# Decayed keys on GpSimd from the seventh tile on, and products of r and k in written order on VectorE

## The chip, the cores and the metric

One NeuronCore of a Trainium2 chip runs the whole program. The metric is the device time of one execution in microseconds (us), lower being better. Engines are called TensorE (PE in the profile), VectorE (DVE), ScalarE (ACT), GpSimd (POOL) and SyncE (SP, which issues the loads and stores).

## The reference

Three layers follow one another on 4 sequences of 768 tokens: a linear attention with decay (8 heads of 48), a gated mixer with a convolution of three taps, and a mixer with layer norm and a residual.

```python
for t in range(S):                                   # attention, S = 768, D = 48
    cur = np.einsum('bhd,bhe->bhde', u[None] * kt, vt)
    y[:, :, t] = np.einsum('bhd,bhde->bhe', rt, state + cur)
    state = w[None, :, :, None] * state + np.einsum('bhd,bhe->bhde', kt, vt)
h = np.maximum(x @ w_in, 0.0)                        # x: 3072 x 384, w_in: 384 x 1024
conv_out = conv_w[0] * h[s-1] + conv_w[1] * h[s] + conv_w[2] * h[s+1]
x = (h / (1 + np.exp(-conv_out))) @ w_out            # w_out: 1024 x 384
xn = (x - mu) / np.sqrt(var + 1e-06) * g_ln
out = x + np.maximum(xn @ w_ch1, 0.0) @ w_ch2        # 384 x 1536 x 384
```

All is float32. The state of the attention after a token is a sum of older keys times values, each weighted by a power of the decay w.

## The kernel before

The tokens are cut into 24 tiles of 128, six to a sequence; tile numbers in the code start at 0, so the seventh tile is n = 6. Within a tile the recurrence becomes matmuls. Per tile these steps are written, and their names are those of the trace:

- `load_tile` (line 224) loads three tensors through SyncE: `kt` (keys by token), `rk` (r and k transposed, 112 x 1024) and `rv` (r and v by token). `rk` and `rv` have three buffers and `kt` two; tile n + 3 is loaded at the end of tile n.
- `decayed_k` (line 244) multiplies the keys by a table and writes `kks`: from the seventh tile on two copies at once, 128 x 768 (line 249), one weighted for the state and one by u. It is called for tile n + 2 at the end of tile n, and `kks` has two buffers, by parity of n.
- `attn_tile` (line 341), first part: the product of r and k with a table of powers, in place on `rk` (line 347, "the product" below); then `av`, the u-weighted keys times r (line 352), its sum over the head (`a`, line 354), and eight ScalarE instructions that put this sum on the diagonal of `aT` (line 358).
- second part: `dot_products` (line 291), eight matmuls of `rk` into `dps`, and two `COPY_PREDICATED` that lay the part of `dps` above the diagonal into `aT` (line 363).
- third part: `products` (line 262), the matmuls into `yps` from state and `aT`; the result is split into a high and a low part `xh` and `xl` (lines 371 and 372), the mixer's input; then the loads and the decayed keys for later tiles.
- `state_update` (line 380): matmuls of `kks` and v into `pst`, and `sn` and `sw`, the new state.

The first six tiles take another way (`light_tile`, line 299) in which the last but one of these parts is spread over GpSimd.

The first mixer works on groups of three tiles: for each of eight blocks of 128 columns nine matmuls into `psm` (weights in a high and a low part, three products of 128 x 128 by 386), ReLU on ScalarE (`h`), the convolution as one ScalarE and two VectorE instructions (`c`, lines 472 and 474), a sigmoid (line 454), a multiply (line 455), and a split into `gh` (ScalarE, line 460) and `gl` (VectorE, line 461). Nine matmuls of these with w_out add up in `acc`, two to three blocks later. The second mixer follows from about 300 us on.

The weights arrive as 64-bit patterns and are decoded on the way (`wjob`, line 139): an absolute value on ScalarE, a clamp on GpSimd (on VectorE for the first four), three integer instructions on VectorE (lines 130 to 135) and a split into a high part (ScalarE: `wih`, `woh`) and a low part (VectorE: `wil`, `wol`). All their instructions carry line 75, that of the helper `InOrder`.

What sets the order: TensorE's instructions are written through `InOrder`, and so keep the order in which they are written. So do the decode's instructions on VectorE, ScalarE and GpSimd among one another (`vo`, `ao`, `go`, lines 78 to 81). Everything that is written with `v_`, `a_` and `g_` is placed by the scheduler of the build, which may move it ahead of or behind other work of its engine.

The attention's parts are put in between the mixer's blocks by `attention` (line 402) and `after1` (line 768); in its steps the first part of tile n + 1 is written after the state update of tile n, and the second part of n + 1 after the third of n.

Of the kernel before, what the change touches and what calls it, by code (L numbers as in the profile page):

```python
# [12 lines left out]
ALU = mybir.AluOpType  # L13
AX = mybir.AxisListType

B, H, S, D = 4, 8, 768, 48
# [21 lines left out]
LIGHT = 6  # L38
# [10 lines left out]
def body(ctx, tc, r, k, v, w, u, w_in, conv_w, w_out, g_ln, w_ch1, w_ch2, rkT, krv, small, out):  # L49
# [13 lines left out]
    v_ = nc.vector  # L63
# [14 lines left out]
    vo = InOrder(nc.vector)  # L78
    ao = InOrder(nc.scalar)
    so = InOrder(nc.sync)  # L80
    go = InOrder(nc.gpsimd)
# [4 lines left out]
    trk = tables_[0:PR, 128:128 + 2 * NP * C].rearrange("x (a p c) -> x a p c", a=2, p=NP)  # L86
# [3 lines left out]
    tku = tables_[:, o + C:o + C + 2 * DM].rearrange("x (a h d) -> x a h d", a=2, h=H)  # L90
# [8 lines left out]
    kks = const.tile([128, 2, 2, H, 64], F32, name="kks")  # L99
# [122 lines left out]
    loaded = {}  # L222

    def load_tile(n):
        if n >= NT:
            return
        rk = io.tile([PR, 2, NP, C], F32, tag="rk", name="rk", bufs=3)
        kt = io.tile([128, DM], F32, tag="k", name="kt", bufs=2)
        rv = io.tile([128, DM + H * 64], F32, tag="rv", name="rv", bufs=3)
        nc.sync.dma_start(out=kt, in_=krv[n, :, 0:DM])  # L230
        nc.sync.dma_start(out=rk.rearrange("x a p c -> x (a p c)"), in_=rkT[n])
        c0 = DM if n < LIGHT else 0
        nc.sync.dma_start(out=rv[:, c0:], in_=krv[n, :, DM + c0:])
        loaded[n] = (rk, kt.rearrange("x (h d) -> x h d", h=H), rv[:, 0:DM].rearrange("x (h d) -> x h d", h=H),
                     rv[:, DM:].rearrange("x (h d) -> x h d", h=H))
# [3 lines left out]
    def new_xT(j):  # L239
        xT[j] = (mp.tile([128, KT, T + 2], F32R, tag="xh", name="xh", bufs=3),  # L240
                 mp.tile([128, KT, T + 2], F32R, tag="xl", name="xl", bufs=3))
        return xT[j]

    def decayed_k(n):

        if n < LIGHT:
            v_.tensor_tensor(out=kks[:, n % 2, 0, :, 0:D], in0=loaded[n][1], in1=tku[:, 0], op=ALU.mult)
            return
        v_.tensor_tensor(out=kks[:, n % 2, :, :, 0:D], in0=loaded[n][1].unsqueeze(1).to_broadcast([128, 2, H, D]), in1=tku,
                         op=ALU.mult)  # L250

    state = [None]
# [9 lines left out]
    def products(n, yps, rT, vt, aT):  # L262
        opened = set()

        def part(g, lhsT, rhs):
            c0 = 32 * (g % 4)
            pe.matmul(yps[c0:c0 + 32, g // 4, :], lhsT=lhsT, rhs=rhs, start=c0 not in opened, stop=True,
                      skip_group_check=True)
            opened.add(c0)

        if n % TPB:
            for g in range(3 * NP):
                p, s_ = divmod(g, 3)
                part(g, sbd[n % 2][:, p, 32 * s_:32 * s_ + 32], rT[:, p, :])
        for parts in zip(*from_heads):
            for g, p, q, c0 in parts:
                pair = vt[:, 2 * p:2 * p + 2, :].rearrange("x a d -> x (a d)")
                part(g, pair[:, c0:c0 + 32], aT[:, q, p, :])

    def halos(n, xh, xl):  # L280
        i, j = n % TPB, n // TT
        for t, e in ((xh, 0), (xl, 1)):
            if i == 0:
                g_.memset(t[:, :, 0:1].bitcast(F32), 0.0)
            if i == TPB - 1:
                g_.memset(t[:, :, T + 1:T + 2].bitcast(F32), 0.0)
            if n % TT == 0 and i > 0:
                g_.tensor_copy(out=xT[j - 1][e][:, :, T + 1:T + 2], in_=t[:, :, 1:2].bitcast(F32))  # L288
                g_.tensor_copy(out=t[:, :, 0:1], in_=xT[j - 1][e][:, :, T:T + 1].bitcast(F32))

    def dot_products(rT, kT):
        dps = [ps_a.tile([128, NP, C], F32, tag="pa", name="dps") for _ in range(2)]
        for p in range(NP):
            for q in range(2):
                q0 = 64 * q
                pe.matmul(dps[q][:, p, :], lhsT=kT[q0:q0 + D, p, :], rhs=rT[q0:q0 + D, p, :], start=True, stop=True)
        return dps

    def light_tile(n, rk, vt, py, py_tag):
# [31 lines left out]
        if n + 2 < NT:  # L331
            decayed_k(n + 2)
# [8 lines left out]
    def attn_tile(n):  # L341
        b, i = divmod(n, TPB)
        rk, _, rt, vt = loaded[n]
        py, py_tag = (ps_c, "acc") if n < EARLY else (ps_a, "pa")

        rT, kT = rk[:, 0], rk[:, 1]
        v_.tensor_tensor(out=rk, in0=rk, in1=trk, op=ALU.mult)  # L347
        if n < LIGHT:
            yield from light_tile(n, rk, vt, py, py_tag)
            return  # L350
        av = ap.tile([128, H, D], F32, tag="av", name="av", bufs=2)
        v_.tensor_tensor(out=av, in0=kks[:, n % 2, 1, :, 0:D], in1=rt, op=ALU.mult)  # L352
        a8 = sp.tile([128, H, 1], F32, tag="a8", name="a8", bufs=2)
        v_.tensor_reduce(out=a8.rearrange("x (q p) o -> x q (p o)", q=2), in_=av.rearrange("x (p q) d -> x q p d", q=2),
                         axis=AX.X, op=ALU.add)
        aT = ap.tile([128, 2, NP, C], F32, tag="aT", name="aT", bufs=2)
        for h in range(H):
            a_.activation(out=aT[:, h // NP, h % NP, :], in_=ident, func=AF.Copy, scale=a8[:, h, :])  # L358
        yield

        dps = dot_products(rT, kT)
        for q in range(2):
            v_.copy_predicated(out=aT[:, q], mask=later.bitcast(I32).unsqueeze(1).to_broadcast([128, NP, C]), data=dps[q])  # L363
        yield

        yps = py.tile([128, KT, C], F32, tag=py_tag, name="yps")
        products(n, yps, rT, vt, aT)
        j = n // TT
        xh, xl = xT[j] if j in xT else new_xT(j)
        sl = slice(1 + (n % TT) * C, 1 + (n % TT) * C + C)  # L370
        a_.activation(out=xh[:, :, sl], in_=yps, func=AF.Copy)
        v_.tensor_tensor(out=xl[:, :, sl], in0=yps, in1=xh[:, :, sl].bitcast(F32), op=ALU.subtract)
        load_tile(n + 3)
        if n + 2 < NT:
            decayed_k(n + 2)
        halos(n, xh, xl)
        finished[0] = n
        yield
# [23 lines left out]
    def attention():  # L402

        tiles = {}

        def go_on(n):
            if 0 <= n < NT:
                next(tiles.setdefault(n, attn_tile(n)), None)

        go_on(0)  # L410
        decayed_k(1)
        go_on(0)
        go_on(1)
        for n in range(NT):
            state_update(n)
            go_on(n - 1)
            if n + 1 != EARLY:
                go_on(n + 1)
            yield
            go_on(n)  # L420
            go_on(n + 2 if n + 1 < EARLY else n + 1)
            yield
# [455 lines left out]
```

## Time and profile before

| | us |
|---|---|
| median of 3 runs (661.33 to 667.29) | 661.51 |
| the profiled execution | 661.62 |
| its span on the core | 659.8 |
| TensorE busy in the span | 627.7 |
| VectorE busy | 416.3 |
| ScalarE busy | 301.8 |
| GpSimd busy | 104.6 |

The profile comes from one execution, taken by the hardware profiler. The span runs from the first to the last instruction; the device time holds 1.8 us more around it. "Busy" is the time in which an engine works on at least one instruction; a share of the whole span is an average over stages that have different limits, so the stretches below are read one by one. A wait is put down to the instruction or load whose end came last before the waiting one began.

### The profile page before, as it was taken

Reading aid. Unit: us, or ns where it says so; the run is one execution under the profiler, and the core shown is the slowest. Engines: PE = TensorE matmul, PEld = TensorE weight load, DVE = VectorE, ACT = ScalarE, POOL = GpSimd, SP = SyncE. Lnnn points to the kernel's source line nnn. Section 1 sums busy time; section 2 is a strip of 40 time slices with the busy share of each in tenths; the row PEclk is TensorE's granted clock in tenths of the full one; section 3 lists DMA queues with packets and bytes.
Section 4 is the critical chain, followed back from the end, with each engine's and each line's share of the span. In section 5 each row is a group of like instructions: output and inputs, shape, how many; then the busy total and the mean of one; then the engine's idle time right before and its main releaser. Section 6 shows DMA issues by size and latency. Waiting matters only on the chain.

```text
span 659.8 us, 11761 instructions
## 1 busy us (share of the span) xinstructions
PE 627.7 (95%) x4782; PEld 574.4 (87%) x4782; DVE 416.3 (63%) x772; ACT 301.8 (46%) x662; POOL 104.6 (16%) x124
## 2 busy tenths in 40 slices
PE   5979699999999999999999999999999999999996
PEld 4868598888988998999998999999999999999995
DVE  6779999999898899877978843413422422422111
ACT  3456868687677778856764521211211221121110
POOL 5464450010001002003115500100100100100000
PEclk9987989999999999999999999999999999999999
DMA  8556716345254332203144303003001101100101
GB/s 250 158 188 208 220 43 208 95 118 160 69 143 158 120 103 63 84 2 132 37 144 132 95 1 96 0 1 96 0 1 49 48 1 49 48 1 13 36 1 52
DMA packets 25295, 56.50 MB, mean 86 GB/s; under 512 B 2961, under 2 KB 15378, under 8 KB 25234
## 3 DMA queue, kind: packets, MB, share of 16 engines
q1 hardware_dynamic: 25234, 55.68, 27.0%
q8 instruction: 39, 0.64, 0.4%
q14 instruction: 22, 0.18, 0.1%
HBM read 46.24 MB, written 9.44 MB: 84 GB/s over the span
## 4 chain that ended last, share of the span: by engine, by line
PE 69%; DVE 14%; DMA 10%; ACT 4%; issue 2%; POOL 1%; SPq 1%; ACTq 0%; DVEq 0%
PE acc L75 32%; PE psm L75 31%; DMA rk<-in_rkT_dram 8%; DVE wdec L75 3%; PE yps L75 3%; DVE c L474 2%; DVE rk L347 2%; ACT aT L358 1%; DVE aT L363 1%; PE pxt L75 1%; PE dps L75 1%; DVE gl L461 1%; DVE c L455 1%; DMA x1b<-x_dram 1%; DVE av L352 1%
## 5 line engine op out<-in xcount | busy, mean ns | idle before, releaser
L488 DVE SCALAR_TENSOR_TENSOR rl<-psm,rh 128x512 fp32r<-128x512 f32 x72 | 49.6, 688 | 132.6 <-ACT rh L487 129.1
L487 ACT ACTIVATE rh<-psm 128x512 fp32r<-128x512 f32 x72 | 43.0, 597 | 186.5 <-PE psm L75 186.5
L75 PE MATMUL acc<-c2h,rh 128*128 128x384 f32 x288 | 97.1, 337 | 0.0
L75 PE MATMUL acc<-c2l,rh 128*128 128x384 f32 x288 | 97.0, 337 | 0.0
L75 PE MATMUL acc<-c2h,rl 128*128 128x384 f32 x288 | 97.0, 337 | 0.0
L75 PE MATMUL psm<-xnh,c1h 128*128 128x512 f32 x216 | 86.5, 401 | 0.0
L75 PE MATMUL psm<-xnh,c1l 128*128 128x512 f32 x216 | 84.9, 393 | 0.0
L75 PE MATMUL psm<-xnl,c1h 128*128 128x512 f32 x216 | 84.8, 393 | 0.0
L474 DVE SCALAR_TENSOR_TENSOR c<-h,tables,c 128x384 f32<-128x384 f32 x128 | 79.4, 626 | 4.8 <-ACT c L472 4.2
L75 PE MATMUL psm<-xh,wih 128*128 128x386 f32 x192 | 69.9, 364 | 4.0 <-DVE aT L363 3.0
L75 PE MATMUL acc<-woh,gh 128*128 128x384 f32 x192 | 66.6, 347 | 3.3 <-ACT woh L75 3.3
L75 PE MATMUL acc<-woh,gl 128*128 128x384 f32 x192 | 65.8, 343 | 3.9 <-DVE gl L461 3.9
L75 PE MATMUL psm<-xl,wih 128*128 128x386 f32 x192 | 67.0, 349 | 2.4 <-POOL xl L288 2.4
L75 PE MATMUL acc<-wol,gh 128*128 128x384 f32 x192 | 65.4, 340 | 1.7 <-DVE wol L75 1.7
L75 PE MATMUL psm<-xh,wil 128*128 128x386 f32 x192 | 66.9, 349 | 0.0
L75 POOL TENSOR_SCALAR wdec<-wdec 128x768 f32<-128x768 f32 (+2 forms) x19 | 54.2, 2851 | 74.2 <-ACT wdec L75 47.4
L75 PEld LDWEIGHTS acc<-c2l,rh 128*128 128x128 f32 x288 | 54.1, 188 | 3.0
L75 PEld LDWEIGHTS acc<-c2h,rh 128*128 128x128 f32 x288 | 54.1, 188 | 2.8
L75 PEld LDWEIGHTS acc<-c2h,rl 128*128 128x128 f32 x288 | 54.1, 188 | 0.0
L511 POOL TENSOR_TENSOR rs<-rs,nhalf 128x1 f32<-128x1 f32 x24 | 16.8, 708 | 210.0 <-DVE rs L510 203.7
L75 PEld LDWEIGHTS psm<-xnh,c1l 128*128 128x128 f32 x216 | 40.6, 188 | 9.2
L75 PEld LDWEIGHTS psm<-xnl,c1h 128*128 128x128 f32 x216 | 40.7, 188 | 6.2
(115 smaller groups left out, 1130.1 us busy)
## 6 DMA issues: line engine op xcount, KB each, us to landing
rk<-in_rkT_dram SPq DMA_DIRECT2D x24, 448.0 KB, 5.0
st<-in_moe_w_ch_dram SPq DMA_DIRECT2D x12, 768.0 KB, 5.9
rv<-in_krv_dram SPq DMA_DIRECT2D x18, 448.0 KB, 4.8
kt<-in_krv_dram SPq DMA_DIRECT2D x24, 192.0 KB, 2.8
x_dram<-x SPq DMA_DIRECT2D x24, 192.0 KB, 1.9
x1b<-x_dram SPq DMA_DIRECT2D x24, 192.0 KB, 3.7
out_dram<-x1b SPq DMA_DIRECT2D x24, 192.0 KB, 2.0
st<-in_moe_w_in_dram SPq DMA_DIRECT2D x6, 512.0 KB, 6.5
```

Source lines behind the costliest of these rows:

```text
L75: return lambda *args, **kw: tc.keep_in_program_order(op(*args, **kw))
L347: v_.tensor_tensor(out=rk, in0=rk, in1=trk, op=ALU.mult)
L352: v_.tensor_tensor(out=av, in0=kks[:, n % 2, 1, :, 0:D], in1=rt, op=ALU.mult)
L358: a_.activation(out=aT[:, h // NP, h % NP, :], in_=ident, func=AF.Copy, scale=a8[:, h, :])
L363: v_.copy_predicated(out=aT[:, q], mask=later.bitcast(I32).unsqueeze(1).to_broadcast([128, NP, C]), data=dps[q])
L455: v_.tensor_tensor(out=st["c"], in0=st["h"][:, 1:T + 1], in1=st["c"], op=ALU.mult)
L461: v_.tensor_tensor(out=st["gl"], in0=st["c"], in1=st["gh"].bitcast(F32), op=ALU.subtract)
L474: v_.scalar_tensor_tensor(out=c, in0=h[:, o:o + T], scalar=cw[:, tap, f:f + 1], in1=c, op0=ALU.mult, op1=ALU.add)
L487: a_.activation(out=gh[:, 0:cols], in_=ps[:, 0:cols], func=AF.Relu)
L488: v_.scalar_tensor_tensor(out=gl_[:, 0:cols], in0=ps[:, 0:cols], scalar=0.0, in1=gh[:, 0:cols].bitcast(F32), op0=ALU.max, op1=ALU.subtract)
L511: g_.tensor_tensor(out=rs[:, 1:2], in0=rs[:, 0:1], in1=nhalf, op=ALU.pow)
```

## The change

The decayed keys of the tiles from the seventh on are written for GpSimd, in written order, in place of VectorE. The product of r and k stays on VectorE, and from the seventh tile on it is written through `InOrder`, so that it keeps its place among VectorE's other written-order instructions (those of the decode).

```diff
         if n < LIGHT:
             v_.tensor_tensor(out=kks[:, n % 2, 0, :, 0:D], in0=loaded[n][1], in1=tku[:, 0], op=ALU.mult)
             return
-        v_.tensor_tensor(out=kks[:, n % 2, :, :, 0:D], in0=loaded[n][1].unsqueeze(1).to_broadcast([128, 2, H, D]), in1=tku,
+        go.tensor_tensor(out=kks[:, n % 2, :, :, 0:D], in0=loaded[n][1].unsqueeze(1).to_broadcast([128, 2, H, D]), in1=tku,
                          op=ALU.mult)
...
         rT, kT = rk[:, 0], rk[:, 1]
-        v_.tensor_tensor(out=rk, in0=rk, in1=trk, op=ALU.mult)
+        (v_ if n < LIGHT else vo).tensor_tensor(out=rk, in0=rk, in1=trk, op=ALU.mult)
         if n < LIGHT:
```

TensorE's order is the same before and after; those of VectorE, ScalarE, GpSimd and SyncE are dealt anew by the scheduler, as the following places show.

VectorE, around the thirteenth tile's `COPY_PREDICATED` (`aT<-tables,dps`), before. `rk<-rk,tables` is the product, L474, L455 and L461 are the mixer's gate:

```order
L455 TENSOR_TENSOR c<-h,c 128x384
L474 SCALAR_TENSOR_TENSOR c<-h,tables,c 128x384
L461 TENSOR_TENSOR gl<-c,gh 128x384
L455 TENSOR_TENSOR c<-h,c 128x384
L372 TENSOR_TENSOR xl<-yps,xh 128x3x128
L347 TENSOR_TENSOR rk<-rk,tables 112x1024
L363 COPY_PREDICATED aT<-tables,dps 128x512 x2
L461 TENSOR_TENSOR gl<-c,gh 128x384
L347 TENSOR_TENSOR rk<-rk,tables 112x1024
L474 SCALAR_TENSOR_TENSOR c<-h,tables,c 128x384
L249 TENSOR_TENSOR kks<-kt,tables 128x16x48
```

The same place of VectorE in the changed order (the product now has line 75, since the helper records it):

```order
L75 TENSOR_TENSOR rk<-rk,tables 112x1024
L352 TENSOR_TENSOR av<-kks,rv 128x384
L455 TENSOR_TENSOR c<-h,c 128x384
L474 SCALAR_TENSOR_TENSOR c<-h,tables,c 128x384
L354 TENSOR_REDUCE a_1898<-av 128x8
L474 SCALAR_TENSOR_TENSOR c<-h,tables,c 128x384
L461 TENSOR_TENSOR gl<-c,gh 128x384
L372 TENSOR_TENSOR xl<-yps,xh 128x3x128
L363 COPY_PREDICATED aT<-tables,dps 128x512 x2
```

Before, the products of the fifteenth and sixteenth tile stand around the thirteenth tile's `COPY_PREDICATED`; now the thirteenth tile's own product stands eight rows ahead of it, with `av` of the fourteenth tile behind it, and the decayed keys are gone.

VectorE, around the seventh tile's `COPY_PREDICATED`, before; `wdec` and `wol` belong to the decode of w_out's first rows that are still missing:

```order
L75 TENSOR_SCALAR wdec<-wdec 128x768
L363 COPY_PREDICATED aT<-tables,dps 128x512
L75 SCALAR_TENSOR_TENSOR wdec<-st,wdec 128x768
L363 COPY_PREDICATED aT<-tables,dps 128x512
L347 TENSOR_TENSOR rk<-rk,tables 112x1024
L75 SCALAR_TENSOR_TENSOR wdec<-st,wdec 128x768
L455 TENSOR_TENSOR c<-h,c 128x384
L474 SCALAR_TENSOR_TENSOR c<-h,tables,c 128x384
L347 TENSOR_TENSOR rk<-rk,tables 112x1024
L75 TENSOR_TENSOR wol<-wdec,woh 128x768
```

From the same `TENSOR_SCALAR` in the changed order; a `gl`, a `c`, the sum of `av` and then `wol` follow on the last row:

```order
L75 TENSOR_SCALAR wdec<-wdec 128x768
L75 TENSOR_TENSOR rk<-rk,tables 112x1024
L455 TENSOR_TENSOR c<-h,c 128x384
L474 SCALAR_TENSOR_TENSOR c<-h,tables,c 128x384
L75 SCALAR_TENSOR_TENSOR wdec<-st,wdec 128x768
L461 TENSOR_TENSOR gl<-c,gh 128x384
L455 TENSOR_TENSOR c<-h,c 128x384
L363 COPY_PREDICATED aT<-tables,dps 128x512
L75 SCALAR_TENSOR_TENSOR wdec<-st,wdec 128x768
L363 COPY_PREDICATED aT<-tables,dps 128x512
L352 TENSOR_TENSOR av<-kks,rv 128x384
```

Before, the two products there are those of the ninth and tenth tile, and the seventh tile's ran some thirty-five rows earlier; now the seventh tile's own product stands right behind the `TENSOR_SCALAR`.

GpSimd, the same stretch, as the difference of the two orders; `wdec` is the clamp of the decode, L314 and L318 belong to the sixth tile:

```order
 L75 TENSOR_SCALAR wdec<-wdec 128x512
+L75 TENSOR_TENSOR kks<-kt,tables 128x16x48
 L314 AFFINE_SELECT aT<-aT 128x512 x2
 L318 TENSOR_TENSOR va<-rv,a_745 128x384
 L75 TENSOR_SCALAR wdec<-wdec 128x512
-L75 TENSOR_SCALAR wdec<-wdec 128x768 x3
+L75 TENSOR_SCALAR wdec<-wdec 128x768 x2
+L75 TENSOR_TENSOR kks<-kt,tables 128x16x48 x2
+L75 TENSOR_SCALAR wdec<-wdec 128x768
```

The seventh tile's keys come ahead of the sixth tile's selects, and those of the eighth and ninth between two clamps.

## Rows read from the trace of the kernel before

**Rows 1.** The page's busy times: busy us (share of the span) and instructions.
```profile
PE 627.7 (95%) x4782; PEld 574.4 (87%) x4782; DVE 416.3 (63%) x772; ACT 301.8 (46%) x662; POOL 104.6 (16%) x124
```
**Rows 2.** Stretches: length, busy us (x) of PE, PEld, DVE, ACT, POOL, PEclk, DMA share, GB/s.
```profile
46.00:89.00 43.00, 34.64 (x294) 31.43 (x290) 38.48 (x62) 29.16 (x67) 24.30 (x18) 0.84 0.61 192
89.00:290.00 201.00, 195.03 (x2138) 179.08 (x2137) 182.70 (x324) 151.40 (x370) 16.59 (x27) 1.00 0.36 111
290.00:652.00 362.00, 360.95 (x1928) 331.81 (x1927) 159.54 (x319) 102.00 (x185) 40.31 (x32) 1.00 0.14 45
```
**Rows 3.** TensorE's waits from 89 to 290 us: us in total, times, longest.
```profile
PE psm L75 <- DVE aT L363: 3.0, 3, 1.3
PE acc L75 <- DVE gl L461: 2.9, 4, 1.5
```
**Rows 4.** VectorE's waits in the same stretch, the longest in total.
```profile
DVE rk L347 <- DMA rk<-in_rkT_dram: 9.7, 10, 2.1
```
**Rows 5.** Timeline at 149 us: start us, us, engine, instruction, [idle before <-releaser].
```profile
149.51 1.23 DVE L347 TENSOR_TENSOR rk<-rk,tables 112x1024 f32<-112x1024 f32 x1 [2.06 <-DMA rk<-in_rkT_dram]
...
150.65 1.34 DVE L363 COPY_PREDICATED aT<-tables,dps 128x512 f32<-128x512 int32 x2
...
151.43 0.45 PE L75 MATMUL psm<-xh,wih 128*128 128x386 f32 x1 [0.97 <-DVE aT L363]
```
**Rows 6.** TensorE's waits from 46 to 89 us, those for the weights w_out.
```profile
PE acc L75 <- ACT woh L75: 3.3, 1, 3.3
...
PE acc L75 <- DVE wol L75: 1.7, 1, 1.7
```
**Rows 7.** VectorE's groups by shape: busy us, mean ns of one | idle before.
```profile
L347 DVE TENSOR_TENSOR rk<-rk,tables 112x1024 f32<-112x1024 f32 x24 | 29.4, 1228 | 15.0 <-DMA rk<-in_rkT_dram 14.6 <-POOL tables L685 0.3
...
L249 DVE TENSOR_TENSOR kks<-kt,tables 128x768 f32<-128x768 f32 x18 | 17.2, 955 | 2.0 <-DMA kt<-in_krv_dram 2.0
...
L352 DVE TENSOR_TENSOR av<-kks,rv 128x384 f32<-128x384 f32 x18 | 10.5, 584 | 0.0
```
**Rows 8.** GpSimd's groups by shape, the two nearest to the key product.
```profile
L75 POOL TENSOR_SCALAR wdec<-wdec 128x768 f32<-128x768 f32 x15 | 47.3, 3155 | 69.0 <-ACT wdec L75 42.2 <-PE psm L75 26.8
...
L318 POOL TENSOR_TENSOR va<-rv,a 128x384 f32<-128x384 f32 x6 | 6.3, 1045 | 0.2 <-ACT a L316 0.2
```
**Rows 9.** Timeline: instructions of VectorE that ran while GpSimd worked.
```profile
64.02 1.18 DVE L352 TENSOR_TENSOR av<-kks,rv 128x384 f32<-128x384 f32 x1
...
139.05 3.09 POOL L75 TENSOR_SCALAR wdec<-wdec 128x768 f32<-128x768 f32 x1 [7.01 <-ACT wdec L75]
...
140.68 0.55 DVE L352 TENSOR_TENSOR av<-kks,rv 128x384 f32<-128x384 f32 x1
```
**Rows 10.** Timeline: `dps` of the ninth and last tile, and VectorE's instruction named with each.
```profile
100.30 1.16 PE L75 MATMUL dps<-rk 48*128 48x128 f32 x16
...
102.50 0.55 DVE L455 TENSOR_TENSOR c<-h,c 128x384 f32<-128x384 f32 x1
...
280.32 1.27 DVE L474 SCALAR_TENSOR_TENSOR c<-h,tables,c 128x384 f32<-128x384 f32 x2
...
281.79 1.16 PE L75 MATMUL dps<-rk 48*128 48x128 f32 x16
```
**Rows 11.** Timeline from the seventh tile's `dps` to the weights that TensorE waits for.
```profile
69.15 1.16 PE L75 MATMUL dps<-rk 48*128 48x128 f32 x16
...
69.67 3.13 POOL L75 TENSOR_SCALAR wdec<-wdec 128x768 f32<-128x768 f32 x1 [2.69 <-ACT wdec L75]
...
73.31 0.55 DVE L75 TENSOR_SCALAR wdec<-wdec 128x768 int32<-128x768 int32 x1
...
80.95 0.95 DVE L75 TENSOR_TENSOR wol<-wdec,woh 128x768 fp32r<-128x768 f32 x1
...
81.95 0.69 PE L75 MATMUL acc<-wol,gh 128*128 128x384 f32 x1 [1.68 <-DVE wol L75]
```
**Rows 12.** The stretch from 80 to 90 us, columns as in rows 2.
```profile
80.00:90.00 10.00, 8.32 (x57) 7.81 (x59) 9.88 (x16) 5.55 (x13) 6.15 (x1) 0.66 0.30 97
```

## The prediction

> **What bounds the kernel now.** I read the stretches first. TensorE is busy for 95% of the span [rows 1], so whatever this change does can only touch the idle time that is left. From 290 us on TensorE has 1 us of idle time in 362; both operations that the change moves are over by then, and nothing is to be had there. In the 201 us before that it is idle for 6.0, and in the 43 us from 46 to 89 for 8.4 [rows 2]. Ahead of 46 us the changed lines don't act: the first decayed keys that move are those of the seventh tile.
>
> Next, who ends those idle times. From 89 to 290 us it is VectorE alone: 3.0 us in three waits for a `COPY_PREDICATED` (line 363) and 2.9 us in four waits for a `gl` (line 461) [rows 3]. VectorE is busy for 182.7 of the 201 us [rows 2], and 9.7 us of its 18.3 idle ones are ten waits in front of the product of r and k, for the load of `rk` [rows 4]. So an engine that sets the pace stands still for a load, while work for TensorE lies ready behind it. The timeline shows one such place in full: the product of the fifteenth tile waits 2.06 us and starts at 149.51, the `COPY_PREDICATED` of the thirteenth follows at 150.65, and TensorE's `psm` matmul waits 0.97 us for it [rows 5]. From 46 to 89 us the large idle time is one place, where the first matmuls of an `acc` block wait 3.3 us for ScalarE's `woh` and 1.7 us for VectorE's `wol`, that is for decoded weights [rows 6].
>
> **The change part by part.** The sum is made against the profiled execution, 661.6 us with a span of 659.8 (1.8 us lie around it); the median of the runs shown, 661.51, is the same to 0.1.
>
> *Keys to GpSimd.* VectorE loses 18 instructions of 0.955 us [rows 7], 17.2 us in all; 16 of them lie from 82 us on, so the middle stretch loses about 15.3. GpSimd gets them. No row shows a product of 128x768 on GpSimd. By length it is twice the `va` product of 128x384, 2 x 1.045 = 2.1 us, and the clamp of 128x768 takes 3.16 [rows 8]. Between 2.1 and 3.2 I take 2.6 (an estimate): 42 us more in a stretch where GpSimd is busy for 16.6 of 201 [rows 2], so its queue holds. Behind a key product, which waits for the load of `kt` and for the `pst` matmuls two tiles earlier, stand only halo copies and the next clamp; `av`, its reader, comes most of a tile later, and the load of the next `kt`, which waits for the key product as before, has a tile as well. All that costs nothing as long as GpSimd does not fall a tile behind.
>
> What GpSimd's work costs VectorE has to be bounded from both sides. An `av` that ran beside GpSimd at 64.02 took 1.18 us against a mean of 0.584: a loss of 0.6. An `av` inside the clamp of 139.05 to 142.14 took 0.55: no loss [rows 7, 9]. I take 0.3 a time, 4.8 for the sixteen. VectorE's work in the middle stretch becomes 182.7 - 15.3 + 4.8 = 172 us of 201.
>
> *Products in written order, middle stretch.* 24 products of 1.228 us stay on VectorE [rows 7]. In the changed order the product of a tile no longer stands ahead of the `COPY_PREDICATED` of two tiles earlier, but behind that of the tile before, among gate work. Its load has then long landed, so I take all of the 9.7 us of waits away. The three waits of TensorE for `COPY_PREDICATED` had a product right ahead of it on VectorE; they go: -3.0 us (bounds 0 and -3.0). The waits for `gl` come from VectorE's backlog, which falls by 15.3 + 9.7 - 4.8 = 20 us over the stretch; I take two thirds of 2.9: -2.0 (bounds 0 and -2.9).
>
> *What is late next.* The product is now close to its own reader, the `dps` matmuls. In the changed order the ninth tile's product stands behind a gate multiply (line 455) that ended at 103.05 in the trace of before; at that pace the product would end at 104.28, and its `dps` started at 100.30, 3.98 earlier. For the twenty-fourth tile the same reading gives 281.59 + 1.23 = 282.82 against 281.79: 1.03 late [rows 10]. Read in this way all sixteen tiles from the ninth on are late, by 0.2 to 4.8 us, 26.7 together. That is at the pace of before. Per tile VectorE gains 0.955 - 0.3 + 9.7/16 = 1.26 us; at the ninth tile it is ahead by some 3 (two key products, the tenth tile's product that before had run already, and a waiting time), and from the tenth or eleventh on by more than the lateness. I take one wait of 1.0 at the ninth tile: +1.0 (bounds 0 and 26.7).
>
> *46 to 89 us.* The seventh tile is where the late product bites. Before, its product ran well ahead, and `dps` started at 69.15 without a wait. Now it stands behind the `TENSOR_SCALAR` on 128x768 weights that started at 73.31, behind GpSimd's clamp of 69.67 to 72.80 [rows 11]. VectorE has less ahead of that instruction (two key products, two products, one `av` with its sum: about 5.5 us), but the clamp waits for ScalarE, so I let it come forward by 2.5 only (an estimate between 0 and 5.5): start 70.8, product over at about 72.2, `dps` 3.0 us late (bounds 0.4 and 5.9). That wait is paid where the 5.0 us of waits for weights were. From the `TENSOR_SCALAR` to the end of `wol` VectorE took 8.6 us (73.31 to 81.90) [rows 11]. The new order has six instructions of `av`'s size more there and one product less; each starts 0.09 before the one ahead ends [rows 5], so 8.6 + 6 x 0.49 - 1.1 = 10.4, and `wol` ends at 81.2 where TensorE went on at 81.95 before: -0.8 (bounds -5.0 if the waits for weights go and nothing comes for them, +3 if both stay). The granted clock was 0.66 from 80 to 90 us, after those idle times [rows 12]: matmuls ran at the lower of the two levels (1.2 GHz) for a while. With 3 us idle at 69 and about 1 at 80 I expect about the same loss, and put nothing down for it.
>
> Sum: -3.0 - 2.0 + 1.0 - 0.8 = -4.8, so 661.6 - 4.8 = 656.8 us.
>
> **Rivals.** *All of it goes* (650.6): the late product of the seventh tile costs nothing net, the waits for weights vanish (-5.0) and so do the 6.0 us of the middle. For it: VectorE's relief of 20 us is more than three times the 6.0 it has to win. Against it: the clamp ahead of the seventh tile's product hangs on ScalarE and a weight load, not on VectorE.
>
> *The products come late on every tile* (669, the other side): place, the `dps` matmuls of the ninth to twenty-fourth tile; price, the 26.7 us worked out above. Each wait also gives VectorE time to catch up, so half, 13.4, less the 6.0 that go: 661.6 + 7.4 = 669. It decides if VectorE's lag behind `psm` stays above 3 to 4 us, that is, if the lag comes from the exchange with ScalarE, step by step, and not from backlog. For it: all sixteen tiles are late at the old pace. Against it: 20 us of relief.
>
> *VectorE is shut out while GpSimd works* (670). Rows 9 speak against it: two-input instructions of VectorE start and end within a clamp. If it were so, each key product would hold VectorE for 2.1 to 3.2 us in place of 0.955: 182.7 - 15.3 + 16 x 2.6 = 209 us of work in 201, 8 us over, so 670. The Trainium skill (SBUF — State Buffer, "Who interferes with whom") states such a rule: a VectorE instruction with two SBUF inputs and a GpSimd instruction that reads SBUF exclude each other for a whole instruction, and whichever was issued first wins. By that rule the `av` at 140.68 would have started at 142.14, so here the trace does not agree.
>
> *It doesn't reach TensorE* (661.5): the waits change names (other late `gl`, other late weights) and the sum stays. For it: most of TensorE's waits are short and spread, and the whole order of VectorE is dealt anew.
>
> **How the numbers follow.** The forecast has 0.50, its own range being 653.5 to 660; all of it goes 0.20; no effect 0.13; late on every tile 0.12; shut out 0.05. One per cent is 6.6 us, about what a measurement of this kernel can tell from no change: 654.9 and 668.1. Faster is the 0.20 and 0.15 of the forecast's 0.50, its lower end: 0.35. Slower is most of the last two cases: 0.14. Within 1% stays 0.51. The range from 650 to 664 leaves out the late cases and the lowest tenth.
>
> **What would show it.** Right: waits of the product for the load of `rk` gone from VectorE, waits of TensorE for `COPY_PREDICATED` gone; VectorE at about 172 us from 89 to 290; GpSimd's key products at 2 to 3.2 us; one wait of TensorE in front of the seventh tile's `dps`, about 3 us, with the wait for `woh` gone and that for `wol` near 1. Wrong: waits in front of many `dps`, named after the product; `av` waiting for GpSimd; VectorE's ordinary instructions lengthened; or waits for `gl` as before.

## The result, and the profile after

The changed kernel took 671.19 us (median of 6 runs, 670.06 to 673.95) against 662.41 for the kernel before (6 runs, 661.33 to 667.29) in the same comparison: a ratio of 1.0142, 95% interval 1.0119 to 1.0166. It is slower by 1.4%; I had forecast 656.8, and the range ended at 664. The profiled execution took 671.29 us, with a span of 669.5 against 659.8.

First the page's busy times of the changed kernel, as in [rows 1]:

```profile
PE 627.9 (94%) x4782; PEld 574.3 (86%) x4782; DVE 426.4 (64%) x754; ACT 302.8 (45%) x662; POOL 139.0 (21%) x142
```

TensorE is busy for as long as before (627.7). So the longer span is idle time of TensorE: 669.5 - 627.9 = 41.6 us against 659.8 - 627.7 = 32.1, which is 9.5 of the 9.7 us. The line also shows something that should not be there. VectorE has 18 instructions less (754 against 772), worth 17.2 us [rows 7], and is busy for 10.1 us *more* (426.4 against 416.3).

The stretches of the changed kernel, columns as in [rows 2], with two of 10 us:

```profile
46.00:89.00 43.00, 35.71 (x329) 32.66 (x330) 36.35 (x53) 27.70 (x61) 25.45 (x15) 0.84 0.57 180
...
80.00:90.00 10.00, 9.23 (x99) 8.25 (x96) 10.00 (x14) 8.00 (x20) 6.08 (x2) 1.00 0.40 129
...
89.00:99.00 10.00, 5.14 (x20) 3.87 (x21) 10.00 (x18) 8.16 (x19) 2.98 (x3) 0.72 0.09 37
...
89.00:290.00 201.00, 187.77 (x1976) 171.85 (x1975) 185.72 (x300) 145.56 (x359) 45.29 (x41) 0.97 0.36 110
```

From 46 to 89 us the changed kernel stands a little better: 7.3 us idle in place of 8.4. From 89 to 290 us TensorE is idle for 13.2 in place of 6.0, and its granted clock is 0.97 in place of 1.00: in the 10 us from 89 on, where it is idle for almost half, the clock falls to 0.72. VectorE is busy for 185.7 us with 300 instructions, where before it was busy for 182.7 with 324: 0.619 us each in place of 0.564.

VectorE's groups by shape tell which instructions grew. First the kernel before, the three largest groups of gate work (lines 455, 461, 474), which I had not read for the forecast; busy us, mean ns of one, then the idle time before them:

```profile
L474 DVE SCALAR_TENSOR_TENSOR c<-h,tables,c 128x384 f32<-128x384 f32 x128 | 79.4, 626 | 4.8 <-ACT c L472 4.2
...
L461 DVE TENSOR_TENSOR gl<-c,gh 128x384 fp32r<-128x384 f32 x64 | 35.7, 557 | 2.9 <-ACT gh L460 2.2
...
L455 DVE TENSOR_TENSOR c<-h,c 128x384 f32<-128x384 f32 x64 | 35.6, 556 | 7.6 <-ACT c L454 7.2
```

The same groups of the changed kernel, and GpSimd's new one:

```profile
L474 DVE SCALAR_TENSOR_TENSOR c<-h,tables,c 128x384 f32<-128x384 f32 x128 | 89.2, 700 | 10.5 <-ACT c L472 9.8
...
L461 DVE TENSOR_TENSOR gl<-c,gh 128x384 fp32r<-128x384 f32 x64 | 42.9, 671 | 7.5 <-ACT gh L460 7.0
...
L455 DVE TENSOR_TENSOR c<-h,c 128x384 f32<-128x384 f32 x64 | 42.1, 658 | 10.7 <-ACT c L454 10.1
...
L75 POOL TENSOR_TENSOR kks<-kt,tables 128x768 f32<-128x768 f32 x18 | 36.5, 2029 | 70.8 <-PE pst L75 43.9 <-issue 15.5 <-DVE c L474 9.6
```

Instructions that the change does not touch, of the same number and shape, take 9.8 + 7.2 + 6.5 = 23.5 us more. For 18 key products that is 1.3 us each, and more than the 17.2 us that the keys had cost VectorE.

The timeline of the changed kernel shows where the time sits (start us, us, engine, instruction, idle before and its releaser):

```profile
70.50 0.56 DVE L75 TENSOR_SCALAR wdec<-wdec 128x768 int32<-128x768 int32 x1
...
70.96 1.22 DVE L75 TENSOR_TENSOR rk<-rk,tables 112x1024 f32<-112x1024 f32 x1
...
72.24 1.40 PE L75 MATMUL dps<-rk 48*128 48x128 f32 x16 [3.95 <-DVE rk L75]
...
80.56 0.94 DVE L75 TENSOR_TENSOR wol<-wdec,woh 128x768 fp32r<-128x768 f32 x1
...
80.61 3.07 POOL L75 TENSOR_TENSOR kks<-kt,tables 128x768 f32<-128x768 f32 x1 [3.35 <-issue]
...
81.56 0.44 PE L75 MATMUL acc<-wol,gh 128*128 128x384 f32 x1 [0.54 <-DVE wol L75]
...
87.63 1.16 PE L75 MATMUL dps<-rk 48*128 48x128 f32 x16 [0.23 <-issue]
...
145.61 2.78 POOL L75 TENSOR_SCALAR wdec<-wdec 128x768 f32<-128x768 f32 x1 [9.07 <-ACT wdec L75]
...
146.80 0.56 DVE L455 TENSOR_TENSOR c<-h,c 128x384 f32<-128x384 f32 x1 [1.96 <-ACT c L454]
...
148.35 2.22 POOL L75 TENSOR_TENSOR kks<-kt,tables 128x768 f32<-128x768 f32 x1
...
148.83 2.16 DVE L474 SCALAR_TENSOR_TENSOR c<-h,tables,c 128x384 f32<-128x384 f32 x1
...
150.91 1.21 DVE L75 TENSOR_TENSOR rk<-rk,tables 112x1024 f32<-112x1024 f32 x1
...
152.22 1.19 PE L75 MATMUL dps<-rk 48*128 48x128 f32 x7 [3.06 <-issue]
...
172.79 1.95 POOL L75 TENSOR_TENSOR kks<-kt,tables 128x768 f32<-128x768 f32 x1 [10.75 <-PE pst L75]
...
173.10 2.07 DVE L461 TENSOR_TENSOR gl<-c,gh 128x384 fp32r<-128x384 f32 x1
175.09 0.61 DVE L474 SCALAR_TENSOR_TENSOR c<-h,tables,c 128x384 f32<-128x384 f32 x1
...
291.90 1.16 PE L75 MATMUL dps<-rk 48*128 48x128 f32 x16
```

Read the pair at 172.79. GpSimd's key product runs until 174.74. A `gl` on VectorE, 0.56 us when alone, starts 0.31 after it and ends at 175.17, that is 0.43 after the key product's end: it is shown as one long instruction, but it did its work when GpSimd had done its own. The next one takes 0.61 again. The pair at 148.35 is the same (key product over at 150.57, the `c` at 150.99), and there the price reaches TensorE: the product of r and k of the thirteenth tile stands right behind, ends at 152.12, and the tile's `dps` starts at 152.22 after 3.06 us of idle time; about half of these, 1.55 us, is the lengthening of that `c`. The profile writes "issue" for it, but the product's end 0.10 us earlier names the cause. The clamp of 145.61 to 148.39 has one tensor as input: a `c` that starts 1.19 us behind its start and ends inside it takes 0.56.

All 18 key products hold one VectorE instruction each, by 0.57 to 1.68 us; 17 of these belong to the gate, and they end 0.41 or 0.42 us behind the product. It goes both ways: the key product at 80.61 starts 0.05 us behind VectorE's `wol`, which takes its usual 0.94, and is itself shown with 3.07 us, where the shortest of the 18 takes 1.83.

Two waits that the change was to end are ended: no wait of VectorE for the load of `rk` is left from 89 us on [rows 4], and none of TensorE for a `COPY_PREDICATED` [rows 3]. In their place TensorE's waits from 89 to 290 us now read (us in total, times, longest):

```profile
PE dps L75 <- issue: 3.3, 2, 3.1
PE acc L75 <- ACT gh L460: 2.8, 1, 2.8
PE dps L75 <- PE yps L75: 2.6, 4, 1.0
PE acc L75 <- DVE gl L461: 2.6, 2, 2.1
PE acc L75 <- ACT x L496: 1.7, 2, 1.4
```

They are `dps` after a late product (six tiles, 5.9 us; where the profile names `yps`, too, the product ended about 0.10 us before), and `acc` for both halves of a late gate. The last, for ScalarE's `x`, was not followed up. By position, the eighth tile's `dps` starts at 87.63, ahead of before by 2.6 us:

```profile
90.22 1.05 PE L75 MATMUL dps<-rk 48*128 48x128 f32 x14
```

and the twenty-fourth tile's at 291.90, behind [rows 10] by 10.1. The loss between them is 12.7 us: 7.3 of more idle time, and the rest about what a clock of 0.97 takes from 187.8 us of matmuls (5.6, an estimate).

### The profile page after: what moved, and what is told of

It is laid out like the page before. It is cut to its first block, busy times and chain, and to the rows that moved or that the text cites. A ratio compares the mean times of both kernels' runs of the same rounds, so it can differ in the third digit from the quotient of the medians.

```text
span 669.5 us, 11783 instructions
## 1 busy us (share of the span) xinstructions
PE 627.9 (94%) x4782; PEld 574.3 (86%) x4782; DVE 426.4 (64%) x754; ACT 302.8 (45%) x662; POOL 139.0 (21%) x142
## 4 chain that ended last, share of the span: by engine, by line
PE 65%; DVE 21%; ACT 5%; DMA 4%; issue 3%; POOL 1%; SPq 1%; DVEq 0%; ACTq 0%
PE acc L75 30%; PE psm L75 30%; DVE c L474 5%; DVE wdec L75 3%; DVE gl L461 3%; DVE c L455 2%; DMA rk<-in_rkT_dram 2%; PE yps L75 2%; ACT aT L358 2%; PE dps L75 1%; DVE rk L75 1%; PE pxt L75 1%; DVE aT L363 1%; DMA st<-in_moe_w_ch_dram 1%; DVE av L352 1%
## 5 line engine op out<-in xcount | busy, mean ns | idle before, releaser
L474 DVE SCALAR_TENSOR_TENSOR c<-h,tables,c 128x384 f32<-128x384 f32 x128 | 89.2, 700 | 10.5 <-ACT c L472 9.8
L75 POOL TENSOR_SCALAR wdec<-wdec 128x768 f32<-128x768 f32 (+2 forms) x19 | 51.3, 2701 | 70.2 <-ACT wdec L75 65.6
L75 POOL TENSOR_TENSOR kks<-kt,tables 128x768 f32<-128x768 f32 x18 | 36.5, 2029 | 70.8 <-PE pst L75 43.9
L455 DVE TENSOR_TENSOR c<-h,c 128x384 f32<-128x384 f32 x64 | 42.1, 658 | 10.7 <-ACT c L454 10.1
```

The source lines that it names most:

```text
L75: return lambda *args, **kw: tc.keep_in_program_order(op(*args, **kw))
L455: v_.tensor_tensor(out=st["c"], in0=st["h"][:, 1:T + 1], in1=st["c"], op=ALU.mult)
L474: v_.scalar_tensor_tensor(out=c, in0=h[:, o:o + T], scalar=cw[:, tap, f:f + 1], in1=c, op0=ALU.mult, op1=ALU.add)
```

## The experiments

The theory was that a GpSimd product with two SBUF inputs holds VectorE's next two-input instruction until it ends, so that handing over the keys costs VectorE more than it frees. The rival was that the products of r and k, moved next to their readers, are late, as in the forecast's second rival. A third question was whether any GpSimd instruction of that length does it. All ratios are against the kernel before, run on the same chip in the same comparison (661.23 us for the first four runs below; 662.21 for the last three).

**One half of the change alone: the keys.**

```diff
-        v_.tensor_tensor(out=kks[:, n % 2, :, :, 0:D], ...
+        go.tensor_tensor(out=kks[:, n % 2, :, :, 0:D], ...
```

> Only the keys move to GpSimd; the products stay where the scheduler puts them. Theory A (shut out: a two-input instruction of GpSimd holds the next two-input instruction of VectorE until it ends): VectorE's gate instructions lengthen by about 1.3 us for each of the 18 keys, some 22 us in all as in the changed kernel, and the time is above before's: 665 to 672. Theory B (only the late products cost): the gate instructions may lengthen but TensorE does not wait for a product; the time is 654 to 661.

Measured: 675.79 us, ratio 1.0198 (1.0167 to 1.0229), slower than both kernels and above the 665 to 672 of theory A. VectorE's groups in it:

```profile
L474 DVE SCALAR_TENSOR_TENSOR c<-h,tables,c 128x384 f32<-128x384 f32 x128 | 87.6, 686 | 8.6 <-ACT c L472 7.6
...
L461 DVE TENSOR_TENSOR gl<-c,gh 128x384 fp32r<-128x384 f32 x64 | 42.1, 658 | 2.4 <-ACT gh L460 2.1
...
L347 DVE TENSOR_TENSOR rk<-rk,tables 112x1024 f32<-112x1024 f32 x24 | 33.9, 1418 | 11.4 <-DMA rk<-in_rkT_dram 10.9 <-POOL tables L685 0.3
```

The gate groups grow by 8.2 + 6.4 + 2.5 us and the product of r and k by 4.5 (1418 ns against 1228): 21.6 together. Most of the waits for the load of `rk` stay (10.9 us of 14.6 [rows 7]). No `dps` waits for its product; TensorE's longest wait from 89 to 290 us is again for `COPY_PREDICATED`, and longer than before [rows 3]:

```profile
PE psm L75 <- DVE aT L363: 6.5, 3, 4.1
```

So the loss comes with the keys, without any product that is late for its `dps`.

**The other half alone: the products in written order.**

```diff
-        v_.tensor_tensor(out=rk, in0=rk, in1=trk, op=ALU.mult)
+        (v_ if n < LIGHT else vo).tensor_tensor(out=rk, in0=rk, in1=trk, op=ALU.mult)
```

> Only the products take the written order; the keys stay on VectorE. Theory A: no lengthened gate instructions, waits of dps for the product no more than a few us: 657 to 664. Theory B: VectorE has 17 us of keys more than in the changed kernel and the products stand as late, so dps waits as long or longer: 668 to 676.

Measured: 658.12 us, ratio 0.9931 (0.9903 to 0.9958). Its stretch from 89 to 290 us:

```profile
89.00:290.00 201.00, 197.99 (x2159) 182.33 (x2160) 186.17 (x331) 151.64 (x371) 18.78 (x26) 0.99 0.36 111
```

TensorE is idle for 3.0 us there, half of before. Nothing is lengthened: 186.17 us for 331 instructions is 0.562 each, as before (0.564). No wait of VectorE for the load of `rk` is left after 89 us, and TensorE's waits from 46 to 89 us begin with the one late product:

```profile
PE dps L75 <- DVE rk L75: 4.0, 1, 4.0
PE psm L75 <- POOL xl L288: 3.1, 1, 3.1
PE psm L75 <- ACT aT L313: 0.7, 1, 0.7
```

This is the seventh tile. From the ninth tile on no `dps` waits for its product. So the rival falls as a cause of its own. That the late products of the changed kernel are late because of held instructions ahead of them fits this; the rows above show it for the thirteenth tile alone, and there for half of the wait. The two halves also add up: +1.98% and -0.69% make +1.29, beside 1.42 for both.

**GpSimd's share kept, with one tensor as input.** The keys from the seventh tile on are copied by a `tensor_scalar` times 1.0; the table's weighting of those keys is left out.

```diff
-        go.tensor_tensor(out=kks[:, n % 2, :, :, 0:D], in0=loaded[n][1]..., in1=tku, op=ALU.mult)
+        go.tensor_scalar(out=kks[:, n % 2, :, :, 0:D], in0=loaded[n][1]..., scalar1=1.0, scalar2=None, op0=ALU.mult)
```

> As the changed kernel, but GpSimd's key instruction has one tensor input (a multiply by 1.0 in place of the table; the weighting of the keys by the table is left out from the seventh tile on). Theory A: no gate instruction lengthens beside it, VectorE's busy time from 89 to 290 us is 165 to 172, and the time is 655 to 662. Theory B: VectorE's order is that of late products as before, dps waits by some 8 us in all, and the time stays at 668 to 673. If a one-input instruction of this shape shuts VectorE out as well, gate instructions lengthen as in the changed kernel.

Measured: 654.63 us, ratio 0.9899 (0.9872 to 0.9926): 2.4% below the changed kernel's ratio, with an instruction on GpSimd that takes longer. Its groups, GpSimd's and then the largest of the gate:

```profile
L75 POOL TENSOR_SCALAR kks<-kt 128x768 f32<-128x768 f32 x18 | 41.4, 2304 | 63.5 <-PE pst L75 44.9 <-issue 16.5 <-POOL xl L288 1.0
...
L474 DVE SCALAR_TENSOR_TENSOR c<-h,tables,c 128x384 f32<-128x384 f32 x128 | 83.8, 658 | 11.3 <-ACT c L472 10.9
```

The gate groups grow by 4.4 + 0.4 + 0.1 = 4.9 us, 0.27 for each of the 18. Its timeline shows where even that sits:

```profile
232.48 2.13 POOL L75 TENSOR_SCALAR kks<-kt 128x768 f32<-128x768 f32 x1 [10.46 <-PE pst L75]
...
232.48 1.23 DVE L474 SCALAR_TENSOR_TENSOR c<-h,tables,c 128x384 f32<-128x384 f32 x1
...
233.90 0.60 DVE L474 SCALAR_TENSOR_TENSOR c<-h,tables,c 128x384 f32<-128x384 f32 x1
```

An instruction that starts together with it takes 0.62 us longer; the next of that kind starts and ends within GpSimd's, at its usual 0.60. The one-input form is not free of the hold: twelve of the 18 lengthen a VectorE instruction, by 0.38 to 0.62 us. But the eleven gate instructions among these end 0.90 or 0.91 us ahead of GpSimd's end, where beside a product of two tensors they end 0.4 behind it. So it is the two-tensor form that holds VectorE to the end, not the length of GpSimd's work. The two forms differ in their operation as well as in the number of inputs, and no run here separates these. Expectations were missed: some gate instructions do lengthen, the time is just below 655 to 662, and VectorE's busy time from 89 to 290 us came out at 182.2, above the 165 to 172 that I had put down. In a stretch of fixed length a faster kernel does more (320 instructions, against 300 in the changed kernel); the mean of one, 0.569, is the number that answers.

**The suspected cost added to the kernel before.** An extra GpSimd instruction for each key product, into a scratch tile that nothing reads; once a product of two tensors, once a `tensor_scalar`.

```diff
+    scr = const.tile([128, 2, H, D], F32, name="scr")
...
+        go.tensor_tensor(out=scr, in0=loaded[n][1]..., in1=tku, op=ALU.mult)
```

> The kernel before, with an extra two-input key product per tile on GpSimd into a scratch tile that nobody reads; VectorE keeps the keys and the products stay free. Theory A: 18 gate instructions or others lengthen by about 1.3 us each, 20 to 24 us of VectorE's time, and the time is 668 to 680. Theory B: nothing but the order changes: 659 to 664.

> The kernel before with an extra instruction per tile on GpSimd into a scratch tile that nobody reads, as the two-input one of the last call, but with one tensor input. If the number of inputs decides: VectorE's instructions beside it lengthen by 0.6 us at most, 5 to 8 us together, and the time is 661 to 668, far below the 683.6 with two inputs. If any GpSimd work of this length, or the order dealt anew, costs that much: 676 or more.

Measured: two inputs 683.60 us, ratio 1.0322 (1.0287 to 1.0357); one input 667.54 us, ratio 1.0088 (1.0058 to 1.0118). VectorE's groups with two inputs (the same lines, two further down):

```profile
L476 DVE SCALAR_TENSOR_TENSOR c<-h,tables,c 128x384 f32<-128x384 f32 x128 | 93.5, 735 | 7.7 <-ACT c L474 7.3
...
L349 DVE TENSOR_TENSOR rk<-rk,tables 112x1024 f32<-112x1024 f32 x24 | 34.6, 1446 | 10.2 <-DMA rk<-in_rkT_dram 9.2 <-PE yps L75 0.7 <-POOL tables L687 0.3
```

and with one:

```profile
L477 DVE SCALAR_TENSOR_TENSOR c<-h,tables,c 128x384 f32<-128x384 f32 x128 | 83.4, 657 | 6.2 <-ACT c L475 5.8
...
L350 DVE TENSOR_TENSOR rk<-rk,tables 112x1024 f32<-112x1024 f32 x24 | 32.8, 1371 | 11.0 <-DMA rk<-in_rkT_dram 10.7 <-POOL tables L688 0.3
```

The gate groups and the product of r and k grow by 14.1 + 5.2 + 3.0 + 1.4 = 23.7 us with two inputs, and by 4.0 + 3.4 + 0.3 + 0.4 = 8.1 with one. Both sums hold 2.6 us that are not the extra instructions' doing: one product of r and k took 3.80 us at 46.15 (3.79 at 45.30 with one input), before the first of them started (56.70 and 55.95). Without it they are 21.1 and 5.5. The time with two inputs is above the expected 668 to 680; the one with one input is as expected.

No work was taken from VectorE here, and by operation, tile and shape VectorE, ScalarE and TensorE run the same instructions in the same order as in the kernel before. So the price stands alone: 15.6 us of VectorE's time between the two forms, and 2.3% of the whole by the two ratios. Why the one-input form still costs 0.9% of the time is not settled; GpSimd's copy also keeps the buffers of `kt` longer, and that was not taken apart.

**The key product in four pieces.** If GpSimd holds VectorE for one instruction at a time, shorter ones should hold it for less.

```diff
-        go.tensor_tensor(out=kks[:, n % 2, :, :, 0:D], ...
+        for h in range(0, H, 2):
+            go.tensor_tensor(out=kks[:, n % 2, :, h:h + 2, 0:D], ..., in1=tku[:, :, h:h + 2], op=ALU.mult)
```

> The changed kernel with each key product on GpSimd cut into four of 128x192. If a two-input instruction of GpSimd shuts VectorE out until that instruction ends, no gate instruction lengthens by more than a piece, 0.5 to 0.6 us, but several per key product may; the loss per key product is 0.5 to 1.5 us and the time 664 to 672. If VectorE is shut out for GpSimd's whole string of work, single gate instructions still lengthen by 1.3 us or more and the time is 670 to 676.

Measured: 663.87 us, just under the expected 664; ratio 1.0033 (1.0015 to 1.0051), 1.1% better than the changed kernel by the two ratios. Its timeline (GpSimd's row holds all four pieces):

```profile
167.92 4.00 POOL L75 TENSOR_TENSOR kks<-kt,tables 128x192 f32<-128x192 f32 x4 [10.65 <-PE pst L75]
...
168.75 0.96 DVE L476 SCALAR_TENSOR_TENSOR c<-h,tables,c 128x384 f32<-128x384 f32 x1
...
169.63 0.95 DVE L463 TENSOR_TENSOR gl<-c,gh 128x384 fp32r<-128x384 f32 x1
```

The two engines take turns: each VectorE instruction is 0.35 to 0.4 us longer and none is held for 1.5. The gate and the products of r and k grow by 5.3 + 2.8 + 1.2 + 2.2 = 11.5 us in all, half of 23.5. GpSimd pays too: 4.00 us here, and 4 x 0.89 = 3.6 on average, for what took 2.03 in one piece; `av` now waits for the keys, 2.1 us in all from 89 to 290. It is still no gain over leaving the keys on VectorE.

**Written order from the eighth tile on.** The remaining loss of the good half was the seventh tile's late product, 4.0 us; here that tile's product is left to the scheduler.

```diff
+        (v_ if n <= LIGHT else vo).tensor_tensor(out=rk, in0=rk, in1=trk, op=ALU.mult)
```

> Keys on VectorE, products in written order from the eighth tile on; the seventh tile's product stays free. If the 4.0 us wait of the seventh tile's dps is a cost of its own, it goes and the time falls from 658 to 652 to 656. If it only stands in for the waits for the weights w_out, those come back and the time stays at 656 to 661.

Measured: 654.57 us (median of 5 runs), ratio 0.9883 (0.9864 to 0.9903). This beats both kernels. Of TensorE's waits from 46 to 89 us, those for weights:

```profile
PE acc L75 <- DVE wol L75: 1.6, 2, 1.0
PE acc L75 <- ACT woh L75: 1.3, 1, 1.3
```

The wait before `dps` is gone, and of the waits for weights, 1.3 and 1.6 us come back where before had 3.3 and 1.7 [rows 6]. By the two ratios (0.9931 against 0.9883) the late product of the seventh tile costs some 0.5% beyond what it hides. The two intervals touch, the runs are from two chips, and the profiled executions (656.95 and 655.78) lie 1.2 us apart, so this size is not shown.

## Why the prediction was wrong

*The step that failed: what GpSimd's work costs VectorE.* I bounded it by 0 and 0.6 us a time and took 0.3. The 18 products cost the gate alone 1.3 each. With 1.3 in place of 0.3, the sixteen products of the middle stretch cost 20.9 us, not 4.8, and outweigh the 15.3 that leave it: the sign of the part turns.

The price alone does not give the loss: by the forecast's own sum VectorE would have 182.7 - 15.3 + 20.9 = 188 us of work in 201. The sum took its waits from VectorE's total; the rows at 148.35 show one that comes of a single instruction, late for the matmul behind it. Term by term, from 89 to 290 us: the waits for `COPY_PREDICATED` fell by 3.0, as forecast; those for the gate rose by 2.5 (5.4 against 2.9), where -2.0 stood; `dps` waited 5.9 for late products, where +1.0 stood; and 1.7 for `x` stood nowhere. That is 7.1 of the 7.3 us of more idle time. The clock of this stretch had no term; the 5.4 us that remain of the 12.7 are about what 0.97 in place of 1.00 costs.

The rows held the answer, and I read them wrongly. The `av` at 64.02 [rows 9] ran beside another GpSimd instruction, which I did not look up:

```profile
63.53 1.26 POOL L318 TENSOR_TENSOR va<-rv,a 128x384 f32<-128x384 f32 x1
```

This `va` has two inputs and ends at 64.79; the `av` ends 0.41 later, as the `gl` at 173.10 ends 0.43 after its key product. Its loss of 0.6 was not an upper end but what was left of a short `va`. The `av` with no loss, at 140.68, ran inside a clamp, with one input, and had started 1.6 us behind the clamp's start. An instruction that starts earlier in a clamp loses time in the trace of before, too: this `c` took 0.98 us, 0.36 more than its usual 0.62.

```profile
96.00 2.98 POOL L75 TENSOR_SCALAR wdec<-wdec 128x768 f32<-128x768 f32 x1 [2.65 <-ACT wdec L75]
...
96.46 0.98 DVE L474 SCALAR_TENSOR_TENSOR c<-h,tables,c 128x384 f32<-128x384 f32 x1
```

I averaged two different things into a price per time. By chance 0.3 is about what the one-input form costs (0.27), and that kernel came to 654.63.

*The rival "shut out".* It had a chance of 0.05 and gave 670; the time was 671.2. Its mechanism is the one that the experiments show, with a smaller size: 1.3 us for a product of 2.03 and not all of 2.6. What is lost is what is left of the product when the VectorE instruction starts: 1.68 us for a `c` that starts with its product (160.17 and 160.21), 0.57 for a `gl` that starts 1.15 us behind it (197.42 and 196.27). That 670 and 671.2 lie so close is luck: with 1.3 in it, this rival's sum gives 188 us of work in 201 and no loss. My reason against it was the clamp of rows 9. The Trainium skill (SBUF — State Buffer, "Who interferes with whom") states the lock between a two-input VectorE instruction and a GpSimd instruction that reads SBUF. The trace agrees for GpSimd's products of two tensors (173.10 to 175.17 behind 172.79 to 174.74), and not in full for its one-input forms, which hold VectorE only at their start (96.46 before) and let later two-input instructions run inside (146.80, and 233.90 without the table). I had let the exception speak against the whole rule.

*Key products on GpSimd.* 2.6 us forecast, 2.03 measured, just under the lower bound of 2.1. GpSimd's queue held, as forecast; only the price on the other engine was wrong.

*VectorE at 172 us from 89 to 290.* 185.7, by the lengthening above; and fixed stretches mislead once kernels run at different paces.

*Waits for the load of `rk`, and for `COPY_PREDICATED`.* Right: both are gone. Without the keys, written order gives 0.69%, some 4.6 us; the terms for it were -3.0 - 2.0 + 1.0 - 0.8 = -4.8. That these agree is in part chance: with the products alone the waits for the gate stay at 2.9 us (2.6 for `gl`, 0.3 for `gh`) where -2.0 stood, and no `dps` waits where +1.0 stood. That the waits for `gl` would ease was put down to both halves, and in the changed kernel they don't: waits for `gh` and `gl` together are 5.4 us against 2.9 for `gl` before.

*Late products from the ninth tile on.* One wait of 1.0 was forecast at the ninth tile. With the products alone there is none; with the keys moved as well there are late ones at six tiles, 5.9 us in all, the longest 3.06 at the thirteenth, half of it by the `c` held right ahead. The reading behind the 26.7 us, "all sixteen", does not come out again: with the instructions of the two traces matched by their order, what stands ahead of the product had ended in time for seven of the sixteen (for the twenty-fourth at 277.79, 2.8 us early enough), and the other nine are late by 15.4 us together.

*46 to 89 us.* Right in nearly every number: the `TENSOR_SCALAR` at 70.50 (70.8 forecast), the product over at 72.18 (72.2), `dps` waiting 3.95 (3.0), the wait for `woh` gone, that for `wol` 0.54 (about 1), and TensorE going on at 81.56 (81.2). The clock loss was not where I left it: from 80 to 90 us it is 1.00 in place of 0.66 [rows 12], and 0.72 from 89 to 99, after the waits for a late gate.

*What stays open.* How the 12.7 us between the eighth and the twenty-fourth tile divide between late gates, late products and the clock is read from one execution of each kernel; the scheduler deals VectorE's order anew in every variant but the two with a scratch tile, so none of the others changes one wait alone. With the keys alone VectorE's work grows by 21.6 - 17.2 = 4.4 us and the time by some 13; which waits make up the difference was not taken apart. The first 46 us also differ between executions: TensorE's idle time there is 14.1 us after and 10.3 before, with a clock of 1.00 and 0.96 and about the same matmuls (433 and 426). This was not followed up.

## What to carry to other kernels

Before handing a two-tensor operation from VectorE to GpSimd, price it by what it holds on VectorE: where VectorE is saturated with two-input work, count up to the GpSimd instruction's length for each, not the time that VectorE is freed. Take the price from a row of the same form, and look for the GpSimd instruction that ran beside it; a one-input neighbour says little about a two-input one, and an instruction that starts late in it says nothing. An instruction that the scheduler hoists in front of its load could be had back cheaply here by written order; the fastest kernel let the first of them, which has no slack yet, stay free.

## What the runs showed of the hardware

- A gate instruction of VectorE (two inputs, 128x384) beside a GpSimd product of two tensors of 128x768 ends about 0.4 us after that product: 2.07 and 2.16 us in place of 0.56 and 0.62. A longer one ends later (`wdec` at 76.11 in the changed kernel, 1.98 us in place of 0.95, 0.81 after). The profile counts the hold as busy time, so it appears in no list of waits.
- A `TENSOR_SCALAR` of VectorE on integers, with one tensor, was held as well: 1.58 us in place of 0.55, at 114.50 with the keys alone.
- GpSimd waits in its turn when VectorE's instruction is the earlier one: 3.07 us for the key product at 80.61, 1.83 for the shortest.
- A GpSimd instruction of the same shape with one input, though longer (2.30 against 2.03 us on average), costs only 0.27 us a time; it holds VectorE at its start alone (1.23 us in place of 0.60 at 232.48), and the gate instructions so held end 0.9 us ahead of its end.
- Cut into four, the GpSimd product and VectorE's instructions alternate: 11.5 us lost in place of 23.5, with GpSimd at 1.8 times the time.
